# Seven products for the second matrix multiply of a gated feed-forward layer, in fifteen of its forty-eight blocks

## The chip, the core and the metric

The kernel runs on one core of one Trainium2 chip. The metric is the device time of one execution, in microseconds. Times that are compared are medians over several executions; a profile is of one execution.

## What is computed

A frequency filter along the sequence, then a normalisation by row and a gated feed-forward layer. The inputs are 8 sequences of 3008 rows of 256 numbers.

```python
X = np.fft.rfft(x, axis=1)
Y = X * (filt_r + 1j * filt_i)[None, :, :]
y = np.fft.irfft(Y, n=x.shape[1], axis=1)        # (8, 3008, 256)

x = y.reshape(24064, 256)
xn = x / np.sqrt(np.mean(x * x, axis=-1, keepdims=True) + 1e-06) * rms_g
g = xn @ w_gate                                  # 256 -> 1536
val = xn @ w_val                                 # 256 -> 1536
out = (g * (1 / (1 + np.exp(-g))) * val) @ w_out # 1536 -> 256
```

## The kernel before

**The feed-forward layer sets the beat.** A sequence b has six blocks m of up to four groups of 128 rows. A block has 12 slots, one for each piece jt of 128 of the 1536 hidden columns, so there are 8 x 6 x 12 = 576 slots in the list `items`. In a slot, `gv` (L533) makes gate and value of one hidden piece for all four row groups: two accumulating matmuls of 512 columns into pg, two into pv (L546), then SiLU on ScalarE (pg to sg, L550) and the product pv x sg on VectorE (hh, L551). pg and pv have two PSUM buffers each, hh has four buffers in turn. `down` (L554) then multiplies hh by w_out: for each of the four row groups one matmul of 256 columns with a 128 x 128 piece of hh as the weights (L563), accumulated over the 12 slots of the block in the two banks po0 and po1. At the block's end ScalarE and VectorE copy one bank each into o3 (L568, L569), and `o_store` sends it out from SP's queue.

**The filter is three stages of matmuls, spread over those slots.** For each sequence `a_unit` (12 units: matmul psa, copy to t1) is the first transform, and goes through DRAM (`z_store`, `t2_load`). The middle stage has 16 units: `b_unit` (four matmuls psb, then `s_part` on VectorE twice, the multiplication by the filter, L231 and L234), `add_unit` (GpSimd, the sum of the two parts, L268), `yt_load` (a transposing DMA on SP, one for two units) and `bi_unit` (four matmuls psi, ScalarE's copy to uu). `t4_load` transposes uu by DMA. The third stage goes by block: `n_unit` (matmul psn, ScalarE's copy to y), `sq_unit` (row sums of squares on ScalarE, L322), `stat_unit` (the factor rho, on GpSimd), `xt_unit` (GpSimd multiplies y's rows by rho, L340) and `tr_unit` (a transposing DMA on SP, which gives the block's xn).

**The order is written out by hand.** Every engine runs its instructions in the order in which the code issues them. The main loop issues for slot i: `gv` of slot i, then what the planner put into this slot, then `down` of slot i-2. The first `down` of a block is put off by one slot, and comes with the second, so that the banks can be emptied. The planner (`fit`, `norm_plan`, `a_plan`, `b_plan`) counts for each slot what it has put on ScalarE ("A"), VectorE ("V") and the two spare PSUM banks ("M", "B"), and moves a unit to a later slot until it fits. `b_at` gives the wished slots of the 16 middle units of sequence b, with t = 72 (b-1) the first slot of sequence b-1's blocks; `lags` say how much later `bi_unit` comes. The filter of sequence b thus runs in the slots of sequence b-1.

Staging buffers of 8 KB a partition (pool stg, four of them) hold filter and weights at the start, and later y, of which only half the buffer is used.

Of the kernel before, what the change touches and what calls it, by code (L numbers as in the profile page):

```python
# [10 lines left out]
FP32 = mybir.dt.float32  # L11
FP16 = mybir.dt.float16
AXT = mybir.ActivationFunctionType
ALU = mybir.AluOpType
# [6 lines left out]
P = 128  # L21
D = 256
B = 8
DFF = 1536
# [9 lines left out]
XC = 6  # L34
NXC = H // XC
KC = 8


def _make_tables():
# [62 lines left out]
def kernel(  # L102
# [21 lines left out]
    stg = ctx.enter_context(tc.tile_pool(name="stg", bufs=4))  # L124
# [27 lines left out]
    wg = glob.tile([P, 2, DFF], FP16)  # L152
    wv = glob.tile([P, 2, DFF], FP16)
    wo = glob.tile([P, JT, D], FP16)
    gsb = glob.tile([P, 2], FP32)
    hhs = [glob.tile([P, 512], FP16, name="hh%d" % i) for i in range(4)]
    ss3 = [glob.tile([P, 4, 2, P], FP16, name="ss%d" % i) for i in range(3)]
# [4 lines left out]
    seen = glob.tile([P, 4], FP16)  # L162

    st = {b: {"x": {}, "t1": {}, "t2": {}, "s": {}, "yt": {}, "t4": {}, "y": {}, "sq": {},
              "u": {}, "xn": {}} for b in range(B)}

    def raw(src, row, ap):
        return bass.AP(tensor=src.tensor, offset=src.offset + row * D, ap=ap)

    def y_tile():  # L170
        t = stg.tile([P, 2, 4, 256], FP32, tag="stg", name="y")
        return t.rearrange("p a b c -> p (a b c)")[:, 0:1024].rearrange("p (a e) -> p a e", a=2)

    def x_load(b, c):
        t = xp.tile([P, XC, D], FP16, tag="xc", name="xc")
# [127 lines left out]
    def nq(b, m):  # L303
        return 3 if (m == 5 and b % 2 == 0) else 4
# [30 lines left out]
    def xt_unit(b, m):  # L335
# [6 lines left out]
                                in1=rho[:, 0:n].unsqueeze(2).to_broadcast([P, n, D]), op=ALU.mult)  # L342
        st[b]["u"][m] = xt

    def tr_unit(b, m):
# [28 lines left out]
    FR4 = 4  # L374

    def f_load(i, f):
        if i not in fst:
            fst[i] = stg.tile([P, 2, FR4, D], FP32, tag="stg", name="fs")
# [134 lines left out]
    def scale_apply(m, bk):  # L513
# [12 lines left out]
                                    in1=y[:, h, :].rearrange("p (q e t) -> p q e t", q=2, e=2), op=ALU.mult)  # L526
        st[0]["xn"][m] = xn

    SPLIT = ((0, 0, 0), (B - 1, 5, JT - 1))
    hh_of = {}  # L530
    po_of = {}

    def gv(b, m, jt):  # L533
        n = nq(b, m)
        xn = st[b]["xn"][m]
        parts = ((0, 2), (2, 4)) if (b, m, jt) in SPLIT else ((0, n),)
        sg = hp.tile([P, 512], FP16, tag="sg", name="sg")
        hh = hhs[(6 * JT * b + JT * m + jt) % 4]
        made = []
        for q0, q1 in parts:  # L540
            w = (q1 - q0) * P
            pg = psG.tile([P, 512], FP32, tag="pg", name="pg")
            pv = psV.tile([P, 512], FP32, tag="pv", name="pv")
            for ps, wt in ((pg, wg), (pv, wv)):
                for dt_ in range(2):
                    nc.tensor.matmul(ps[:, 0:w], wt[:, dt_, ts(jt, P)], xn[:, q0:q1, dt_, :],  # L546
                                     start=(dt_ == 0), stop=(dt_ == 1))
            made.append((pg, pv, w, slice(q0 * P, q1 * P)))
        for pg, pv, w, c in made:
            nc.scalar.activation(out=sg[:, c], in_=pg[:, 0:w], func=AXT.Silu)  # L550
            nc.vector.tensor_tensor(out=hh[:, c], in0=pv[:, 0:w], in1=sg[:, c], op=ALU.mult)  # L551
        hh_of[(b, m, jt)] = hh
# [36 lines left out]

    def w_load(q):  # L590
        cols = ts(q, DFF // 3)
        t = stg.tile([P, 2, 2, DFF // 3], FP32, tag="stg", name="ws")
# [17 lines left out]
    with tc.manual_schedule():  # L610
# [142 lines left out]
        def norm_plan(b, m, slots, r):  # L753
            for i in range(2):
                s = fit(slots[i], ("M", 0, 1), ("A", 0, 0.6), ("A", 1, 0.82))
                at(s, n_unit, b, m, i)
                at(s + 1, sq_unit, b, m, i)
            for d, fn in zip(r, (stat_unit, xt_unit, tr_unit)):
                at(s + d, fn, b, m)
# [50 lines left out]
        for b in range(1, B):  # L810
            t = (b - 1) * 72
            if b == 1:
                z = a_plan(b, [i for i in range(12)])
                b_at, lags = [z + 7 + 7 * i // 5 for i in range(16)], (9, 9)
                soft = range(2, 16, 4)
            elif b == 2:
                z = a_plan(b, [28 + 3 * i for i in range(12)])
                b_at, lags, soft = [z + 13 + 7 * i // 3 for i in range(16)], (8, 9), ()
            else:
                at_ = [72 + 3 * i if b == 3 else t - 87 + 4 * i for i in range(12)]  # L820
                z = a_plan(b, [s - (s % JT == 1) for s in at_])
                b_at, lags, soft = [t - (25 if b == 3 else 26) + 4 * i for i in range(16)], (8, 12), ()
            assert z + 3 <= b_at[0] - 4
            end = b_plan(b, b_at, lags, soft)
            for c in range(4):
                at(end + 1 + (3 * c if b < 3 else c), t4_load, b, c)
            n_at = end + (4, 6, 8)[b] if b < 3 else t + (53 if b == 3 else 51)
            assert n_at >= end + 4
            for m in range(6):
                norm_plan(b, m, (n_at + 8 * m, n_at + 8 * m + (4 if b > 1 else 2)), (2, 3, 7) if b > 1 else (2, 3, 6))  # L830

        for i, now in plan.items():
            if any(fn == a_unit and a[3] == 0 for fn, a in plan.get(i + 1, ())) and bi_unit in [fn for fn, _ in now]:
                now.sort(key=lambda u: u[0] == sq_unit)

        stores = {}
        for i in range(len(items) + 4):
            if i < len(items):
                gv(*items[i])
            for fn, a in plan.pop(i, ()):  # L840
                fn(*a)
            if 2 <= i < len(items) + 2:
                b, m, jt = items[i - 2]
                if jt == 1 and i > JT:
                    down(b, m, 0)
                if jt or i < JT:
                    down(b, m, jt)
                if items[i - 2][2] == JT - 1:
                    stores[i + 1] = items[i - 2][:2]
# [35 lines left out]
```

## Time and profile before

| | |
|---|---|
| time, median of 3 runs (lowest, highest) | 863.48 us (862.96, 863.52) |
| span of the profiled execution, first to last instruction | 861.4 us |
| granted TensorE clock | 0.999 |
| instructions | 17024 |
| matmuls on TensorE | 6142 |
| data moved by DMA | 107.98 MB, 125 GB/s |
| ScalarE SiLU, L550, 128x512 | 595 ns each |
| VectorE product hh, L551, 128x512 | 691 ns each |
| VectorE filter products, L231 and L234, 128x384 | 547 and 546 ns each |
| GpSimd row scale, L340, 128x1024 | 1893 ns each |
| GpSimd sum of parts, L268, 128x384 | 911 ns each |

How to read it: engines are PE (TensorE's matmuls), PEld (its weight loads, which overlap the matmuls), DVE (VectorE), ACT (ScalarE), POOL (GpSimd) and SP (which only issues DMAs). A group's row has the line, the engine, the operation, what it writes and reads by the program's names, the shapes and the number of instructions; after the first bar the busy time in us and the mean length of one in ns; after the second the idle time of the engine just before them, and what ended it. A row in the order of time has start and length in us; where several instructions are merged, the length goes from the first one's start to the last one's end. A matmul's length includes the way through the array, so that one starts before the last has ended.

### The profile page before, as it was taken

To read this page: it belongs to the slowest core of one execution; us is meant where nothing else is said; L and a number is where in the kernel's file an instruction comes from. 1 tells how busy PE (TensorE), PEld (TensorE's weight loads), DVE (VectorE), ACT (ScalarE), POOL (GpSimd) and SP (SyncE) were. 2 spreads that over 40 slices of the span, in tenths; PEclk is the share of its full clock that TensorE was granted. 3 is DMA by queue.
4 is the path that set the end of the run, shared out by engine and by line. 5 is a ranking of instruction groups with operands and counts; after the bars stand their busy time and mean duration, and the time that the engine had idled before them with its cause. 6 is when DMAs were issued, how large, how long until landed. Compare 5 with 4: busy or idle time off the path is not lost.

```text
span 861.4 us, 17024 instructions
## 1 busy us (share of the span) xinstructions
PE 852.4 (99%) x6142; PEld 532.2 (62%) x6142; DVE 557.2 (65%) x926; ACT 612.4 (71%) x1339; POOL 297.8 (35%) x346
## 2 busy tenths in 40 slices
PE   8999999999999999999999999999999999999997
PEld 6755666566666666666666666666666666665664
DVE  5857655776666666666666676767666665555554
ACT  4986777787588756887577856888567765777443
POOL 5725742453144322534034430444123430132000
PEclk9999999999999999999999999999999999999999
DMA  9995778765975476656755548433564331521101
GB/s 283 270 204 124 150 164 168 139 130 121 197 137 129 121 150 111 151 107 147 139 127 113 132 98 180 108 87 101 131 127 93 97 70 42 124 54 49 62 25 50
DMA packets 198237, 107.98 MB, mean 125 GB/s; under 512 B 158566, under 2 KB 182520, under 8 KB 198152
## 3 DMA queue, kind: packets, MB, share of 16 engines
q1 hardware_dynamic: 189464, 85.52, 44.1%
q0 software_dynamic: 8544, 21.24, 12.7%
q8 instruction: 48, 0.79, 0.4%
q14 instruction: 37, 0.30, 0.1%
q10 hardware_dynamic: 144, 0.13, 0.0%
HBM read 45.78 MB, written 35.65 MB: 95 GB/s over the span
## 4 chain that ended last, share of the span: by engine, by line
PE 96%; DMA 1%; ACT 1%; DVE 1%; issue 0%; POOL 0%; POOLq 0%
PE po L563 28%; PE pg L546 28%; PE pv L546 28%; PE psb L241 3%; PE psi L285 3%; PE psn L314 2%; PE psa L206 2%; DMA fs<-in_filt_i_dram 1%; PE psy L418 1%; PE psf L389 1%; PE pst L367 0%; ACT sg L550 0%; POOL xc L186 0%; DVE s L231 0%; DVE hh L551 0%
## 5 line engine op out<-in xcount | busy, mean ns | idle before, releaser
L551 DVE TENSOR_TENSOR hh<-pv,sg 128x512 f16<-128x512 f32 (+2 forms) x578 | 391.5, 678 | 286.4 <-ACT sg L550 221.9
L550 ACT ACTIVATE sg<-pg 128x512 f16<-128x512 f32 (+2 forms) x578 | 337.4, 584 | 217.6 <-PE pg L546 213.4
L546 PE MATMUL pg<-xn,wg 128*128 128x512 f16 (+2 forms) x1156 | 338.1, 374 | 0.1
L546 PE MATMUL pv<-xn,wv 128*128 128x512 f16 (+2 forms) x1156 | 338.1, 374 | 0.0
L563 PE MATMUL po<-wo,hh 128*128 128x256 f16 x2256 | 332.7, 273 | 0.0
L563 PEld LDWEIGHTS <-hh 128*128 128x128 f16 x2256 | 213.4, 98 | 105.5 <-issue 0.6
L268 POOL TENSOR_TENSOR ss<-s,s 128x384 f16<-128x384 f16 x112 | 101.9, 911 | 273.2 <-DVE s L234 245.2
L546 PEld LDWEIGHTS <-wv 128*128 128x128 f16 x1156 | 112.9, 98 | 130.7
L546 PEld LDWEIGHTS <-wg 128*128 128x128 f16 x1156 | 111.4, 98 | 17.0 <-issue 0.3
L340 POOL TENSOR_TENSOR xt<-y,rho 128x1024 f16<-128x1024 f32 (+1 forms) x46 | 85.4, 1856 | 2.8
L322 ACT ACTIVATE junk<-y 128x256 f16<-128x256 f32 x180 | 74.3, 413 | 2.8
L231 DVE TENSOR_TENSOR s<-psb,ff 128x384 f16<-128x384 f32 x124 | 67.6, 547 | 0.7 <-ACT ff L195 0.6
L234 DVE TENSOR_TENSOR s<-psb,ff 128x384 f16<-128x384 f32 x124 | 67.6, 546 | 0.0
L195 ACT ACTIVATE uu<-psi 128x384 f16<-128x384 f32 (+1 forms) x127 | 61.6, 486 | 1.5 <-DMA out_dram<-o 0.5
L195 ACT ACTIVATE y<-psn 128x512 f32<-128x512 f32 (+1 forms) x95 | 55.7, 588 | 4.2
L285 PEld LDWEIGHTS <-yt 96*128 96x128 f16 x512 | 35.4, 97 | 26.7 <-issue 1.0
L332 POOL TENSOR_TENSOR rho<-u,mhalf 128x4 f32<-128x4 f32 (+1 forms) x46 | 46.5, 1010 | 3.8
L330 POOL TENSOR_SCALAR u<-ss 128x4 f32<-128x4 f32 (+1 forms) x46 | 8.9, 193 | 104.8 <-ACT junk L322 103.8
L195 ACT ACTIVATE t<-psa 128x512 f16<-128x512 f32 x70 | 41.4, 594 | 3.1 <-PE psa L206 1.7
L285 PE MATMUL psi<-wi,yt 96*128 96x96 f16 x512 | 42.9, 205 | 0.1
L241 PE MATMUL psb<-wb,t 96*128 96x96 f16 x480 | 40.1, 206 | 0.3 <-DVE s L234 0.2
L241 PEld LDWEIGHTS <-t 96*128 96x128 f16 x480 | 28.7, 97 | 12.8 <-DVE s L234 3.3
(101 smaller groups left out, 366.2 us busy)
## 6 DMA issues: line engine op xcount, KB each, us to landing
out_dram<-o SPq DMA_DIRECT2D x40, 512.0 KB, 3.6
xc<-in_x_dram POOLq DMA_DIRECT2D x31, 384.0 KB, 5.6
z_tmp<-t SPq DMA_DIRECT2D x28, 384.0 KB, 2.7
t<-z_tmp SPq DMA_DIRECT2D x28, 384.0 KB, 6.0
out_dram<-o SPq DMA_DIRECT2D x7, 384.0 KB, 2.7
fs<-in_filt_i_dram POOLq DMA_DIRECT2D x3, 512.0 KB, 10.8
fs<-in_filt_r_dram POOLq DMA_DIRECT2D x3, 512.0 KB, 11.2
ws<-in_moe_w_gate_dram POOLq DMA_DIRECT2D x3, 512.0 KB, 9.8
```

Source lines behind the costliest of these rows:

```text
L195: nc.scalar.activation(out=out, in_=in_, func=AXT.Copy, **({} if scale is None else {"scale": scale}))
L231: eng.tensor_tensor(out=o, in0=ps, in1=f1, op=ALU.mult)
L234: eng.tensor_tensor(out=o, in0=ps[:, :, ::-1, :], in1=f2, op=ALU.mult)
L241: nc.tensor.matmul(ps[:, ts(k, KR)], st[b]["t2"][kk // KC][:, kk % KC, ds(dh * P, P)], wb[0:KR, kk, :], start=True, stop=True)
L268: nc.gpsimd.tensor_tensor(out=ss3[g % 3][:, :, dh, 0:KR], in0=s[0], in1=s[1], op=ALU.add)
L285: nc.tensor.matmul(ps[:, k, :], yt[0:KR, k, dh, :], wi[0:KR, 4 * g + k, :], start=True, stop=True)
L322: nc.scalar.activation(out=junk, in_=y[:, i, ts(u, D)], func=AXT.Square, accum_out=ss[:, 2 * i + u:2 * i + u + 1])
L340: nc.gpsimd.tensor_tensor(out=xt[:, 0:n, :], in0=y.rearrange("p a (u d) -> p (a u) d", u=2)[:, 0:n, :], in1=rho[:, 0:n].unsqueeze(2).to_br ...
L546: nc.tensor.matmul(ps[:, 0:w], wt[:, dt_, ts(jt, P)], xn[:, q0:q1, dt_, :], start=(dt_ == 0), stop=(dt_ == 1))
L550: nc.scalar.activation(out=sg[:, c], in_=pg[:, 0:w], func=AXT.Silu)
L551: nc.vector.tensor_tensor(out=hh[:, c], in0=pv[:, 0:w], in1=sg[:, c], op=ALU.mult)
L563: nc.tensor.matmul(po[s4 // 2][:, s4 % 2, :], hh[:, ts(s4, P)], wo[:, jt, :], start=(jt == 0 and s4 % 2 == 0), stop=(jt == JT - 1 and (s4 ...
```

## The change

Fifteen blocks get another way through the second multiply: blocks 3 and 4 of the sequences 2 to 6, and blocks 0 to 4 of the last. With the row groups in two halves, `gv_seven` makes two hidden pieces for two row groups in a slot (eight matmuls of 256 columns, with twice the weight loads), SiLU and product as before. hh then holds a 2 x 2 matrix of 128 x 128 tiles, two row groups by two hidden pieces, and w_out's part a 2 x 2 matrix too. Strassen's method (seven products of sums of tiles in place of eight) needs sums of tiles of hh, which `sums` makes on VectorE, sums of tiles of w_out, which `w_seven` makes once on GpSimd, and sums of the products. `down_seven` has seven matmuls of 128 columns in a slot where `down` has four of 256. A half of the block is six slots; at its end results are put together on ScalarE, VectorE and GpSimd. The main loop issues `sums` of slot i-1 at the end of slot i, behind `down` of i-2.

```diff
+    big = [glob.tile([P, 2 * FR4 * D], FP32, name="big%d" % i) for i in range(4)]
+    spare = [t[:, FR4 * D:] for t in big]
+    half = [t.bitcast(FP16) for t in spare]
...
+    def xt_act(b, m, q):
+        rho = st[b]["u"][m]
+        y = st[b]["y"][m].rearrange("p a (u d) -> p (a u) d", u=2)
...
+        nc.scalar.activation(out=st[b]["xt"][m][:, q, :], in_=y[:, q, :], func=AXT.Copy, scale=rho[:, q:q + 1])
...
+    SEVEN = {(b, m) for b in range(2, B - 1) for m in (3, 4)} | {(B - 1, m) for m in range(5)}
+
+    def w_seven(n):
+        v = wo.rearrange("p (i j) (e d) -> p i j e d", j=2, e=2)
+        f, a, b = ((ALU.add, (0, 0), (1, 1)), (ALU.subtract, (0, 1), (1, 1)), (ALU.subtract, (1, 0), (0, 0)),
+                   (ALU.add, (0, 0), (0, 1)), (ALU.add, (1, 0), (1, 1)))[n]
+        nc.gpsimd.tensor_tensor(out=ws7[n], in0=v[:, :, a[0], a[1], :], in1=v[:, :, b[0], b[1], :], op=f)
+
+    def gv_seven(b, m, jt):
+        half, jp = divmod(jt, JP)
...
+        for ps, wt in ((pg, wg), (pv, wv)):
+            for j in range(2):
+                for dt_ in range(2):
+                    nc.tensor.matmul(ps[:, ts(j, 2 * P)], wt[:, dt_, ts(2 * jp + j, P)],
+                                     xn[:, 2 * half:2 * half + 2, dt_, :], start=(dt_ == 0), stop=(dt_ == 1))
+        nc.scalar.activation(out=sg, in_=pg, func=AXT.Silu)
+        nc.vector.tensor_tensor(out=hh, in0=pv, in1=sg, op=ALU.mult)
+
+    def sums(b, m, jt):
+        a = hh_of[(b, m, jt)].rearrange("p (s t) -> p s t", s=4)
...
+        nc.vector.tensor_tensor(out=hs[:, 0:2], in0=a[:, 0:2], in1=a[:, 3:4].to_broadcast([P, 2, P]), op=ALU.add)
+        nc.vector.tensor_tensor(out=hs[:, 2:4], in0=a[:, 1:3], in1=a[:, 0:4:3], op=ALU.subtract)
+        nc.vector.tensor_tensor(out=h5, in0=a[:, 0], in1=a[:, 2], op=ALU.add)
+
+    def down_seven(b, m, jt):
...
+        mm(pb[:, 0], a[:, 0], ws7[1][:, jp], **first)
+        mm(pb[:, 1], a[:, 3], ws7[2][:, jp], **mid)
+        mm(pa[:, 0], hs[:, 0], ws7[0][:, jp], **first)
+        mm(pb[:, 3], hs[:, 1], w[:, 0, 0], **mid)
+        mm(pa[:, 2], hs[:, 2], ws7[3][:, jp], **mid)
+        mm(pa[:, 1], hs[:, 3], ws7[4][:, jp], **last)
+        mm(pb[:, 2], h5, w[:, 1, 1], **last)
+        if jp == JP - 1:
+            o = o3_of[(b, m)][:, 2 * half:2 * half + 2, :].rearrange("p q (e d) -> p (q e) d", e=2)
+            t = osum
+            nc.scalar.activation(out=t[:, 4], in_=pa[:, 0], func=AXT.Copy)
+            nc.scalar.activation(out=t[:, 0:4], in_=pb, func=AXT.Copy)
+            nc.vector.tensor_tensor(out=o[:, 0:4:3], in0=pa[:, 1:3], in1=t[:, 4:5].to_broadcast([P, 2, P]), op=ALU.add)
+            nc.gpsimd.tensor_tensor(out=o[:, 1:3], in0=t[:, 0:2], in1=t[:, 2:4], op=ALU.add)
+            nc.gpsimd.tensor_tensor(out=t[:, 2:4], in0=t[:, 1::-1], in1=t[:, 2:4], op=ALU.subtract)
+            nc.gpsimd.tensor_tensor(out=o[:, 0:4:3], in0=o[:, 0:4:3], in1=t[:, 2:4], op=ALU.add)
...
         w_load(0)
-        w_load(1)
...
+        w_load(1)
         f_neg(4, 4, (0,))
...
+        for b, m in SEVEN:
+            for jt in range(JT):
+                load["V"][6 * JT * b + JT * m + jt] += 0.56
+            load["A"][6 * JT * b + JT * m + JP + 1] += 0.7
...
+            if fast:
+                for q in range(nq(b, m)):
+                    at(s + r[1] + 1 + q, xt_act, b, m, q)
+                    load["A"][s + r[1] + 1 + q] += 0.4
+                r = (0, 0, r[1] + 5)
+            else:
+                at(s + r[1], xt_unit, b, m)
...
-                b_at, lags, soft = [t - (25 if b == 3 else 26) + 4 * i for i in range(16)], (8, 12), ()
+                b_at, lags, soft = [t - 13 + 3 * i for i in range(16)], (8, 11), ()
...
+        for n in range(5):
+            at(96 + 10 * n, w_seven, n)
...
-                gv(*items[i])
+                (gv_seven if items[i][:2] in SEVEN else gv)(*items[i])
...
+                seven = (b, m) in SEVEN
+                fn, n = (down_seven, JP) if seven else (down, JT)
+                if jt % n == 1 and i > JT:
+                    fn(b, m, jt - 1)
+                if jt % n or i < JT:
+                    fn(b, m, jt)
+                if i - 1 < len(items) and items[i - 1][:2] in SEVEN:
+                    sums(*items[i - 1])
+                if jt == JT - 1:
+                    stores[i + (3 if seven else 1)] = (b, m)
```

So the middle stage of the sequences 3 to 7 has a unit every three slots (before, every four), from 13 slots ahead of t (before, 25 or 26), which puts nearly all of it ahead of the blocks 3 and 4. Where a block's row scale would fall into one of the fifteen blocks, `xt_act` does it on ScalarE in four multiplies, one a slot, and the transpose of the block's xn comes later by as much: this is so for 8 blocks. The staging pool becomes four plain buffers used in turn, and their upper halves, which y leaves free, hold the sums of tiles.

More of the change, by code (lines that the diff above doesn't have):

```diff
@@ L36 @@
 KC = 8
+FR4 = 4
 def _make_tables():
@@ L154 @@
     wo = glob.tile([P, JT, D], FP16)
+    big = [glob.tile([P, 2 * FR4 * D], FP32, name="big%d" % i) for i in range(4)]
+    spare = [t[:, FR4 * D:] for t in big]
+    half = [t.bitcast(FP16) for t in spare]
+    ws7 = [half[n // 2][:, ts(n % 2, JT // 2 * P)].rearrange("p (i d) -> p i d", d=P) for n in range(5)]
+    hs4 = [(half[0][:, 1536:], half[1][:, 1536:], half[3][:, 0:512], half[3][:, 512:1024])[i]
+           .rearrange("p (s t) -> p s t", s=4) for i in range(4)]
+    hs1 = [half[3][:, 1024 + i * P:1024 + (i + 1) * P] for i in range(4)]
+    osum = spare[2][:, 384:1024].rearrange("p (s t) -> p s t", s=5)
     gsb = glob.tile([P, 2], FP32)
@@ L164, with big_tile @@
     st = {b: {"x": {}, "t1": {}, "t2": {}, "s": {}, "yt": {}, "t4": {}, "y": {}, "sq": {},
-              "u": {}, "xn": {}} for b in range(B)}
+              "u": {}, "xn": {}, "xt": {}} for b in range(B)}
     def raw(src, row, ap):
         return bass.AP(tensor=src.tensor, offset=src.offset + row * D, ap=ap)
+    turn = [0]
+    def big_tile():
+        turn[0] += 1
+        return big[(turn[0] - 1) % 4]
     def y_tile():
-        t = stg.tile([P, 2, 4, 256], FP32, tag="stg", name="y")
-        return t.rearrange("p a b c -> p (a b c)")[:, 0:1024].rearrange("p (a e) -> p a e", a=2)
+        return big_tile()[:, 0:FR4 * D].rearrange("p (a e) -> p a e", a=2)
     def x_load(b, c):
@@ L343, in xt_unit @@
         st[b]["u"][m] = xt
+    def xt_act(b, m, q):
+        rho = st[b]["u"][m]
+        y = st[b]["y"][m].rearrange("p a (u d) -> p (a u) d", u=2)
+        if q == 0:
+            st[b]["xt"][m] = xtp.tile([P, 4, D], FP16, tag="xt", name="xt")
+        nc.scalar.activation(out=st[b]["xt"][m][:, q, :], in_=y[:, q, :], func=AXT.Copy, scale=rho[:, q:q + 1])
+        if q == nq(b, m) - 1:
+            st[b]["y"].pop(m)
+            st[b]["u"][m] = st[b]["xt"].pop(m)
     def tr_unit(b, m):
@@ new lines, in gv_seven @@
+    def gv_seven(b, m, jt):
+        half, jp = divmod(jt, JP)
+        xn = st[b]["xn"][m]
+        sg = hp.tile([P, 512], FP16, tag="sg", name="sg")
+        hh = hhs[(6 * JT * b + JT * m + jt) % 4]
+        pg = psG.tile([P, 512], FP32, tag="pg", name="pg")
+        pv = psV.tile([P, 512], FP32, tag="pv", name="pv")
+        for ps, wt in ((pg, wg), (pv, wv)):
[5 more added lines that the diff above has]
+        nc.vector.tensor_tensor(out=hh, in0=pv, in1=sg, op=ALU.mult)
+        hh_of[(b, m, jt)] = hh
@@ new lines, in sums @@
+    def sums(b, m, jt):
+        a = hh_of[(b, m, jt)].rearrange("p (s t) -> p s t", s=4)
+        n = (6 * JT * b + JT * m + jt) % 4
+        hs, h5 = hs4[n], hs1[n]
+        nc.vector.tensor_tensor(out=hs[:, 0:2], in0=a[:, 0:2], in1=a[:, 3:4].to_broadcast([P, 2, P]), op=ALU.add)
+        nc.vector.tensor_tensor(out=hs[:, 2:4], in0=a[:, 1:3], in1=a[:, 0:4:3], op=ALU.subtract)
+        nc.vector.tensor_tensor(out=h5, in0=a[:, 0], in1=a[:, 2], op=ALU.add)
+        hh_of[(b, m, jt)] = (a, hs, h5)
@@ new lines, in down_seven @@
+    def down_seven(b, m, jt):
+        a, hs, h5 = hh_of.pop((b, m, jt))
+        half, jp = divmod(jt, JP)
+        if jt == 0:
+            o3_of[(b, m)] = op.tile([P, 4, D], FP32, tag="o3", name="o3")
+        if jp == 0:
+            po_of[(b, m)] = [psO.tile([P, 2, D], FP32, tag="po%d" % i, name="po%d" % i)
+                             .rearrange("p a (e d) -> p (a e) d", e=2) for i in range(2)]
+        pa, pb = po_of[(b, m)]
+        first, mid, last = dict(start=(jp == 0), stop=False), dict(start=False, stop=False), \
+            dict(start=False, stop=(jp == JP - 1))
+        w = wo[:, 2 * jp:2 * jp + 2, :].rearrange("p j (e d) -> p j e d", e=2)
+        mm = nc.tensor.matmul
+        mm(pb[:, 0], a[:, 0], ws7[1][:, jp], **first)
[14 more added lines that the diff above has]
+            nc.gpsimd.tensor_tensor(out=o[:, 0:4:3], in0=o[:, 0:4:3], in1=t[:, 2:4], op=ALU.add)
+            po_of[(b, m)] = o3_of[(b, m)]
@@ L529 @@
     SPLIT = ((0, 0, 0), (B - 1, 5, JT - 1))
+    o3_of = {}
     hh_of = {}
@@ L591, in w_load @@
         cols = ts(q, DFF // 3)
-        t = stg.tile([P, 2, 2, DFF // 3], FP32, tag="stg", name="ws")
+        t = big_tile().rearrange("p (k e j) -> p k e j", k=2, e=2)
         for src, k in ((moe_w_gate, 0), (moe_w_val, 1)):
@@ L757, in norm_plan @@
                 at(s + 1, sq_unit, b, m, i)
-            for d, fn in zip(r, (stat_unit, xt_unit, tr_unit)):
-                at(s + d, fn, b, m)
+            fast = items[s + r[1]][:2] in SEVEN
+            at(s + r[0], stat_unit, b, m)
+            if fast:
[5 more added lines that the diff above has]
+                at(s + r[1], xt_unit, b, m)
+            at(s + r[2], tr_unit, b, m)
             assert s + r[-1] + 1 < 72 * b + 12 * m
@@ L843 @@
                 b, m, jt = items[i - 2]
[L844 to L849, printed above, removed]
+                seven = (b, m) in SEVEN
[8 more added lines that the diff above has]
+                    stores[i + (3 if seven else 1)] = (b, m)
             for fn, a in late.pop(i, ()):
```

5 lines of the change are left out of this document (2 added, 3 removed).

## The prediction

> **What bounds the kernel now.** I read the page's busy shares and its chain first.
>
> ```profile
> PE 852.4 (99%) x6142; PEld 532.2 (62%) x6142; DVE 557.2 (65%) x926; ACT 612.4 (71%) x1339; POOL 297.8 (35%) x346
> ...
> PE 96%; DMA 1%; ACT 1%; DVE 1%; issue 0%; POOL 0%; POOLq 0%
> ```
>
> TensorE is busy and is the chain; other engines matter only where one makes it wait. Next, one slot in the order of time (start, length):
>
> ```profile
> 609.97 0.69 DVE L551 TENSOR_TENSOR hh<-pv,sg 128x512 f16<-128x512 f32 x1
> 610.01 0.59 PE L546 MATMUL pg<-xn,wg 128*128 128x512 f16 x2
> 610.44 0.60 PE L546 MATMUL pv<-xn,wv 128*128 128x512 f16 x2
> 610.64 0.60 ACT L550 ACTIVATE sg<-pg 128x512 f16<-128x512 f32 x1 [0.70 <-PE pg L546]
> 610.87 0.60 PE L563 MATMUL po<-wo,hh 128*128 128x256 f16 x4
> 611.27 0.69 DVE L551 TENSOR_TENSOR hh<-pv,sg 128x512 f16<-128x512 f32 x1 [0.61 <-ACT sg L550]
> ```
>
> The next pg starts at 611.31, so a slot is 1.30 us. A 512-column matmul takes 0.216 (610.01 to 610.44 is two), a 256-column one 0.109 ((0.60 - 0.273)/3): 4 x 0.216 + 4 x 0.109 = 1.30. From pg's start to SiLU is 0.63, from SiLU to hh another 0.63. `down` uses an hh two slots old, so these latencies cost nothing now. Then, what the new instructions can be priced by, from the groups by shape:
>
> ```profile
> L551 DVE TENSOR_TENSOR hh<-pv,sg 128x512 f16<-128x512 f32 x526 | 363.3, 691 | 265.9 <-ACT sg L550 207.3 <-PE psn L314 28.9 <-PE psa L206 13.4
> ...
> L551 DVE TENSOR_TENSOR hh<-pv,sg 128x256 f16<-128x256 f32 x4 | 1.6, 422 | 1.0 <-ACT sg L550 0.8 <-PE pg L546 0.2
> ...
> L197 DVE COPY t4f<-pst 128x512 f16<-128x512 f16 x1 | 0.4, 425 | 0.5 <-PE pst L434 0.5
> ...
> L510 DVE TENSOR_TENSOR hl<-rho,hl 128x4 f16<-128x4 f32 x1 | 0.2, 163 | 0.0
> ```
>
> VectorE takes 1.05 ns an element from fp32 ((691 - 422)/256) over about 0.158 fixed, but 0.52 from fp16 ((425 - 158)/512). An operation that waits for nothing starts before the last has ended:
>
> ```profile
> 500.77 0.69 DVE L551 TENSOR_TENSOR hh<-pv,sg 128x512 f16<-128x512 f32 x1
> 501.38 0.55 DVE L231 TENSOR_TENSOR s<-psb,ff 128x384 f16<-128x384 f32 x1
> ```
>
> 0.61 from start to start, 0.08 less than the length. And the two places that show 128-column matmuls with a weight load each, and a load that waits for VectorE:
>
> ```profile
> 47.59 0.65 PEld L483 LDWEIGHTS <-t 128*128 128x128 f16 x8
> 47.80 0.61 PE L483 MATMUL psn<-tab,t 128*128 128x128 f16 x8
> ```
>
> ```profile
> 23.31 1.02 DVE L231 TENSOR_TENSOR s<-psb,ff 128x384 f16<-128x384 f32 x2 [0.64 <-ACT ff L195]
> ...
> 23.92 0.17 PEld L418 LDWEIGHTS <-s 128*96 128x96 f16 x2 [1.03 <-DVE s L231]
> 23.92 0.26 PE L418 MATMUL psy<-tab,s 128*96 128x128 f16 x1 [0.79 <-DVE s L231]
> ```
>
> Eight take 0.61, the last 0.219 of it: (0.61 - 0.219)/7 = 0.056 each. The first multiply ends at 23.31 + 0.55 = 23.86, the load starts 0.05 later, and its matmul lasts 0.26 where others last 0.22: 0.09 from VectorE's end to useful work.
>
> **The change, part by part.** The sum is made against the profiled execution, 861.4 us; the median of the runs, 863.5, lies 2.1 above it, which I add at the end.
>
> *TensorE's columns.* In a seven-product slot gate and value are 8 matmuls of 256 columns, 0.872, and seven products of 128 are 7 x 0.056 = 0.392: 1.264 in place of 1.300. Fifteen blocks are 180 slots: 180 x 0.036 = -6.5 us, the most there is to gain.
> [...]
>
> *Operand sums.* VectorE gets two additions of 256 fp16 elements and one of 128 per slot, SBUF to SBUF. No row shows that form. At fp16's 0.52 they last 0.158 + 0.134 = 0.292 and 0.225; at fp32's 1.05, 0.427 and 0.292. I take the fp16 end: the nearest row with fp16 in and out is L197's. Less 0.083 of overlap they take 0.209 + 0.209 + 0.142 = 0.56; with hh's 0.61 VectorE has 1.17 of 1.264, so it fits as a sum. In time it doesn't. The code issues hh of slot i ahead of the sums of i-1, and `down_seven(i-1)` comes one slot later, behind that slot's gate and value. From the start of slot i: gate's fourth matmul ends 3 x 0.109 + 0.272 = 0.60; SiLU starts at 0.64, hh at 1.27 (+0.63), the sums at 1.88 (+0.61); the last ends 0.418 + 0.225 later, 2.52, and its matmul can run at 2.61. TensorE gets to that matmul at 1.264 + 0.872 + 6 x 0.056 = 2.47. So it waits 0.14; that lengthens the slot, so the next sum is in time: 0.14 every second slot.
>
> *Half blocks.* Results now leave PSUM every 6 slots, not 12. The postponed pair of `down`s gives TensorE two slots' gates in a row, and VectorE has no such gap: counted from the slot with the half's last product, hh issues 1.27 to 1.88; the new addition out of PSUM (256 elements, 0.422 - 0.083 = 0.34) waits for ScalarE's first copy, to 2.25; sums to 2.81. ScalarE's copies (128 and 512 elements: 0.28 and 0.595, overlapping by 0.1) start at 1.60, when the last product lands, so SiLU starts at 2.28 and hh at 2.90; the sums end at 4.15, usable at 4.24. TensorE wants them at 1.40 + 2 x 0.872 + 0.392 + 0.336 = 3.87: 0.37 late. With the waits in the other slots (the fourth and the sixth of the half) a half loses 0.37 + 2 x 0.14 = 0.64 and gains 6 x 0.036 = 0.22: +0.42, by 30 halves **+12.6 us**.
>
> *Costed at nothing.* ScalarE's row scale: 8 blocks, 32 multiplies of 256 (0.41 each by L322) in place of 8 GpSimd ones of 1.89; between two SiLUs ScalarE has 0.7 idle (the slot above). Uncovered: 32 x 0.41 = 13 us. Other planned work in these slots (15 groups of psi at 0.17, 16 of psn at 0.22) gives VectorE time while its copies take some of ScalarE's: -3 to +3, taken as 0. The middle stage at three slots a unit, with its transposes and loads on SP in the same order: the planner put batch 2's at 7/3 slots before, and there TensorE hardly waited:
>
> ```profile
> 150.00:205.00 55.00, 54.89 (x404) 33.05 (x403) 39.49 (x68) 42.85 (x97) 27.61 (x29) 1.00 0.63 128
> ```
>
> 0.11 idle in 55 bounds five batches (36 slots each, 234 us) to +0.5; uncovered, each of 80 units could hold TensorE for one s multiply, 0.46: 37 us. Five weight sums on GpSimd (768 elements; L340 takes 1466 ns for as many), ten slots apart, sit in its idle 65%; late, they would hold an add, the yt transpose behind it on SP and psi, 8 us in all. The store on SP now waits three slots for GpSimd, and t4 and yt loads queue behind it; psi has five slots, 6.5 us, against yt's 3.2 to land. The second weight load keeps its place in GpSimd's queue.
>
> Sum: 861.4 + 12.6 = 874.0, + 2.1 = **876 us**. Its own range is 867 to 885: 0.05 us a slot either way over 180 slots.
>
> **Rivals.**
> 1. *The sums wait behind GpSimd.* After each half GpSimd makes three dependent additions of 256 fp32 elements; L340's 1893 ns for 1024 and 1466 for 768 give 1.67 an element, 0.61 each. If an addition keeps VectorE's two-input SBUF operations waiting, one met in the two groups of sums there holds everything behind it: 30 x 0.61 = 18, so **894**. For it: the adds fall on those sums. Against it: nothing shown; VectorE has no such two-input pair at work beside GpSimd before.
> [...]
> 2. *A rate binds.* Sums at 1.05 an element take 0.90, VectorE 1.51 + 0.34/6 = 1.56 a slot: 180 x 0.26 = +47, **911**. Seven loads of 0.098 uncovered (0.69 for 0.39) come to the same. Against: L197's fp16 copy; L483's 56 ns.
> 3. *The sums are ready in time* (faster). Place: the last sum of each slot, 0.14 late in a chain of 2.6, and the 0.37 at the half. If the chain to it is shorter by these, by a smaller fixed part (a 4-element memset takes 62 ns) and a SiLU not held by the copies, only the columns count: 861.4 - 6.5 + 2.1 = **857**. It decides from waits under 0.22 a half.
> 4. *It cancels*: the fixed part alone shrinks to 62. The steady wait goes, the half's falls to about 0.25: 30 x (0.25 - 0.22) = +1, **864**.
>
> **Chances.** Forecast 0.46, port 0.20, rate 0.06, in time 0.20, cancels 0.08. A measurement of this kernel can tell 0.2%, 1.7 us: faster 0.20, same 0.08, slower 0.72. The range 857 to 897 takes in 3 and 4 and most of 1, and leaves out 2 and 1's upper part.
>
> **What would show it.** Seven matmuls of 128 columns in 0.39 us when not held; sums of 0.29 and 0.22 us; idle TensorE ended by VectorE's sums, some 0.6 us a half, most behind the postponed pair; blocks without seven products unchanged. Sums far longer where GpSimd's additions run would show rival 1; sums of 0.43 rival 2; a TensorE without waits in those blocks makes the prediction wrong.

## The result, and the profile after

| | before | after |
|---|---|---|
| time, median of 4 runs | 863.45 us | 905.82 us (904.80 to 907.31) |
| ratio, 95% interval | | 1.0494 (1.0481 to 1.0507) |
| span of the profiled execution | 861.4 us | 904.1 us |
| granted TensorE clock, mean | 0.999 | 0.997 |

The changed kernel is slower by 42.4 us, above the predicted range of 857 to 897. Shares and chain of its page:

```profile
PE 868.2 (96%) x7402; PEld 603.9 (67%) x7402; DVE 679.0 (75%) x1477; ACT 632.8 (70%) x1420; POOL 361.6 (40%) x433
...
PE 76%; DVE 12%; ACT 5%; issue 4%; DMA 2%; SPq 1%; POOL 0%; ACTq 0%; DVEq 0%; POOLq 0%
```

VectorE holds 12% of the chain, where it had 1%. GpSimd is not in the chain at all, although, as will be seen, it causes most of the loss: it doesn't release TensorE, it lengthens what VectorE does. Who makes TensorE wait (total us, times, longest), from the view of waits:

```profile
PE po L600 <- DVE big L580: 11.2, 27, 0.5
PE po L602 <- DVE big L581: 8.1, 15, 1.6
PE po L604 <- DVE big L582: 5.5, 13, 0.6
```

L580 to L582 are the three operand sums; L598 to L604 are the seven products. The groups by shape:

```profile
L581 DVE TENSOR_TENSOR big<-hh 128x256 f16<-128x256 f16 x180 | 67.4, 374 | 0.0
L582 DVE TENSOR_TENSOR big<-hh 128x128 f16<-128x128 f16 x180 | 52.3, 290 | 0.0
L580 DVE TENSOR_TENSOR big<-hh 128x256 f16<-128x256 f16 x180 | 51.7, 287 | 0.0
...
L611 POOL TENSOR_TENSOR o<-big 128x256 f32<-128x256 f32 x30 | 24.0, 801 | 134.1 <-ACT big L609 134.1
L613 POOL TENSOR_TENSOR o<-o,big 128x256 f32<-128x256 f32 x30 | 23.0, 768 | 2.4
L612 POOL TENSOR_TENSOR big<-big 128x256 f32<-128x256 f32 x30 | 22.8, 760 | 2.4
```

L580 (an addition) and L581 (a subtraction) have the same shape and follow each other at once, yet one takes 287 ns on average and the other 374. The end of a half in the order of time shows why (the products' weight loads and some matmuls are left out):

```profile
803.25 0.43 DVE L610 TENSOR_TENSOR o<-po,big 128x256 f32<-128x256 f32 x1 [0.18 <-ACT big L608]
...
803.60 0.28 DVE L580 TENSOR_TENSOR big<-hh 128x256 f16<-128x256 f16 x1
803.73 0.75 POOL L611 TENSOR_TENSOR o<-big 128x256 f32<-128x256 f32 x1 [9.02 <-ACT big L609]
803.79 0.84 DVE L581 TENSOR_TENSOR big<-hh 128x256 f16<-128x256 f16 x1
...
804.56 0.79 POOL L612 TENSOR_TENSOR big<-big 128x256 f32<-128x256 f32 x1
...
804.69 0.68 DVE L573 TENSOR_TENSOR hh<-pv,sg 128x512 f16<-128x512 f32 x1
...
805.29 0.28 DVE L580 TENSOR_TENSOR big<-hh 128x256 f16<-128x256 f16 x1
805.43 0.72 POOL L613 TENSOR_TENSOR o<-o,big 128x256 f32<-128x256 f32 x1
805.49 0.81 DVE L581 TENSOR_TENSOR big<-hh 128x256 f16<-128x256 f16 x1
805.62 0.23 PE L600 MATMUL po<-big,big 128*128 128x128 f16 x1 [0.46 <-DVE big L580]
...
806.36 0.23 PE L602 MATMUL po<-big,big 128*128 128x128 f16 x1 [0.45 <-DVE big L581]
```

L581 begins 0.06 us after GpSimd's first addition, and lasts 0.84 in place of 0.28, to 0.15 after the addition's end. The same happens with the third addition. The second runs beside hh (L573), which reads PSUM and one SBUF operand, and hh keeps its 0.68. TensorE, which has two slots' products in a row here, waits for L580 and then for L581.

**An account of the 42.7 us of span.** I add up, over all pairs of successive matmuls, what lies from start to start beyond 0.216, 0.109 and 0.056 us for 512, 256 and 128 columns (0.163 for 384). Before, these waits are some 3 us after the start-up; after, they are 37.5 in the fifteen blocks and 14.8 in the others. 37.5 + 11.8 more, less 6.3 of saved columns, is 43.0. A block counts here from its first gate matmul to that of the next block, so the products of its last two slots fall into the block behind it: of the 14.8 us, 8.0 are still waits of seven-product matmuls, which wait 45.5 us in all.

Most of the loss stands in one place. The two slots of a block that hold the postponed pair are 2.57 and 3.03 us long on average, and 1.73 and 1.72 without the sums (experiment 3). The products of these slots wait 31.5 us in all. In the six halves that follow no additions, because a normal block stands in front, it is 0.33 to 0.35 us each; in the other 24 halves it is 0.82 to 1.36.

### The profile page after: what moved, and what is told of

Same layout as the page of the kernel before. It is cut to its first block, busy times and chain, and to the rows that moved or that the text cites. A ratio compares the mean times of both kernels' runs of the same rounds, so it can differ in the third digit from the quotient of the medians.

```text
span 904.1 us, 20300 instructions
## 1 busy us (share of the span) xinstructions
PE 868.2 (96%) x7402; PEld 603.9 (67%) x7402; DVE 679.0 (75%) x1477; ACT 632.8 (70%) x1420; POOL 361.6 (40%) x433
## 4 chain that ended last, share of the span: by engine, by line
PE 76%; DVE 12%; ACT 5%; issue 4%; DMA 2%; SPq 1%; POOL 0%; ACTq 0%; DVEq 0%; POOLq 0%
PE po L651 17%; PE pg L634 17%; PE pv L634 17%; PE pg L570 5%; PE pv L570 4%; PE psb L254 2%; ACT sg L572 2%; DVE hh L573 2%; DVE big L582 2%; DVE big L581 2%; PE psi L298 2%; PE psa L219 2%; PE psn L327 2%; DVE big L580 1%; PE po L602 1%
## 5 line engine op out<-in xcount | busy, mean ns | idle before, releaser
L639 DVE TENSOR_TENSOR hh<-pv,sg 128x512 f16<-128x512 f32 (+2 forms) x398 | 267.2, 672 | 181.7 <-ACT sg L638 140.0
L638 ACT ACTIVATE sg<-pg 128x512 f16<-128x512 f32 (+2 forms) x398 | 230.4, 580 | 128.0 <-PE pg L634 124.5
L634 PE MATMUL pg<-xn,wg 128*128 128x512 f16 (+2 forms) x796 | 231.5, 372 | 0.1
L634 PE MATMUL pv<-xn,wv 128*128 128x512 f16 (+2 forms) x796 | 231.5, 372 | 0.0
L651 PE MATMUL po<-wo,hh 128*128 128x256 f16 x1536 | 227.3, 272 | 0.0
L281 POOL TENSOR_TENSOR ss<-s,s 128x384 f16<-128x384 f16 x112 | 102.6, 917 | 206.0 <-DVE s L247 189.5
L572 ACT ACTIVATE sg<-pg 128x512 f16<-128x512 f32 x180 | 107.5, 597 | 105.7 <-PE pg L570 94.4
L573 DVE TENSOR_TENSOR hh<-pv,sg 128x512 f16<-128x512 f32 x180 | 123.7, 687 | 24.2 <-ACT sg L572 20.0
L570 PE MATMUL pg<-xn,wg 128*128 128x256 f16 x720 | 108.0, 273 | 0.0
L570 PE MATMUL pv<-xn,wv 128*128 128x256 f16 x720 | 108.0, 273 | 0.0
L634 PEld LDWEIGHTS <-wg 128*128 128x128 f16 x796 | 76.3, 98 | 11.4 <-issue 0.3
L611 POOL TENSOR_TENSOR o<-big 128x256 f32<-128x256 f32 x30 | 24.0, 801 | 134.1 <-ACT big L609 134.1
L335 ACT ACTIVATE junk<-big 128x256 f16<-128x256 f32 x180 | 74.7, 415 | 2.8
L581 DVE TENSOR_TENSOR big<-hh 128x256 f16<-128x256 f16 x180 | 67.4, 374 | 0.0
```

Of the source, the lines that this page charges most:

```text
L281: nc.gpsimd.tensor_tensor(out=ss3[g % 3][:, :, dh, 0:KR], in0=s[0], in1=s[1], op=ALU.add)
L335: nc.scalar.activation(out=junk, in_=y[:, i, ts(u, D)], func=AXT.Square, accum_out=ss[:, 2 * i + u:2 * i + u + 1])
L570: nc.tensor.matmul(ps[:, ts(j, 2 * P)], wt[:, dt_, ts(2 * jp + j, P)], xn[:, 2 * half:2 * half + 2, dt_, :], start=(dt_ == 0), stop=(dt_ = ...
L572: nc.scalar.activation(out=sg, in_=pg, func=AXT.Silu)
L573: nc.vector.tensor_tensor(out=hh, in0=pv, in1=sg, op=ALU.mult)
L581: nc.vector.tensor_tensor(out=hs[:, 2:4], in0=a[:, 1:3], in1=a[:, 0:4:3], op=ALU.subtract)
```

## The experiments

In the order in which they were run; the waits are counted as above.

| kernel | time, us | ratio to before (95%) | waits in the fifteen blocks / others, us |
|---|---|---|---|
| the changed kernel | 905.8 | 1.0494 (1.0481, 1.0507) | 37.5 / 14.8 |
| GpSimd's adds left out | 880.9 | 1.0199 (1.0184, 1.0215) | 13.2 / 13.7 |
| memsets in their place | 881.1 | 1.0202 (1.0187, 1.0217) | 13.2 / 14.2 |
| no operand sums | 859.6 | 0.9954 (0.9939, 0.9969) | 0.1 / 5.8 |
| sums in their hh's slot | 883.1 | 1.0225 (1.0208, 1.0242) | 21.5 / 7.3 |
| middle stage where it was | 916.3 | 1.0614 (1.0596, 1.0632) | 50.4 / 12.6 |
| row scale all on GpSimd | 911.9 | 1.0562 (1.0546, 1.0578) | 47.0 / 11.3 |
| three slots behind | 881.8 | 1.0212 (1.0197, 1.0227) | 8.7 / 19.3 |
| the same, no adds | 871.0 | 1.0089 (1.0074, 1.0104) | 0.4 / 17.6 |
| three behind in the fifteen only | 876.5 | 1.0156 (1.0141, 1.0172) | 9.2 / 13.9 |
| the same, adds paced | 867.2 | 1.0049 (1.0036, 1.0061) | 1.4 / 12.3 |
| two behind, adds paced | 881.5 | 1.0210 (1.0196, 1.0224) | 16.8 / 11.4 |
| sums behind the drain | 878.7 | 1.0179 (1.0165, 1.0193) | 17.0 / 8.5 |
| three behind, paced, bank awaited | 864.5 | 1.0013 (1.0004, 1.0022) | 1.4 / 11.4 |

**1. GpSimd's three additions left out.**

```diff
-            nc.scalar.activation(out=t[:, 0:4], in_=pb, func=AXT.Copy)
-            nc.vector.tensor_tensor(out=o[:, 0:4:3], in0=pa[:, 1:3], ...)
-            nc.gpsimd.tensor_tensor(out=o[:, 1:3], ...)
-            nc.gpsimd.tensor_tensor(out=t[:, 2:4], ...)
-            nc.gpsimd.tensor_tensor(out=o[:, 0:4:3], ...)
+            nc.scalar.activation(out=o, in_=pb, func=AXT.Copy)
+            nc.vector.tensor_tensor(out=t[:, 0:2], in0=pa[:, 1:3], ...)
```

> Left out: GpSimd's three additions at the end of each half (ScalarE's second copy goes straight into the output buffer, VectorE's addition into the scratch), so all else runs as in the changed kernel. Theory A, exclusion: an operand sum, with two inputs in SBUF, and a GpSimd addition that reads SBUF can't run together. Then the second sum's mean falls from 374 ns to about 290, TensorE's wait behind the postponed pair from about 1.3 us to 0.4, and the time by 30 x 0.9 = 27 us to about 879. Theory B, order alone: the waits come from hh being issued ahead of the sums, GpSimd's work beside them is chance; then the time stays at 906, within 3 us.

880.9: the additions cost 24.9 us. The sums take 281, 310 and 218 ns, and the waits at the postponed pairs fall from 31.5 to 7.3 us, while the six halves without additions in front keep their 0.33 to 0.35. The seven products still wait 21.3 us in all. Of this 5.0 us stand at five products behind sums that other GpSimd work lengthens as before: one row scale, and four times L281, the sum of the two filter parts.

**2. Three memsets of 512 elements in place of the additions**, 0.52 us each, which only write.

```diff
+            for _ in range(3):
+                nc.gpsimd.memset(t[:, 0:4], 0.0)
```

> As the run without additions, but with three GpSimd memsets of 512 fp32 elements in their place: GpSimd is at work at the same moments, and only writes SBUF. Theory A, if the shared thing is a way to read: as without the additions, about 879, sums of 290 ns. If any GpSimd work beside them holds the sums: more than 890, with long second sums. Theory B: 906.

881.1, as without anything. The memsets lie on the same sums:

```profile
787.41 0.28 DVE L580 TENSOR_TENSOR big<-hh 128x256 f16<-128x256 f16 x1
787.55 0.53 POOL L612 MEMSET big<- 128x512 f32 x1 [9.03 <-DVE big L610]
787.61 0.28 DVE L581 TENSOR_TENSOR big<-hh 128x256 f16<-128x256 f16 x1
787.81 0.22 DVE L582 TENSOR_TENSOR big<-hh 128x128 f16<-128x128 f16 x1
```

So it isn't GpSimd's being busy that holds the sums (L581 takes 0.28 here, 0.84 beside an addition): what the memsets lack against the additions is the reading of SBUF.

**3. No operand sums**; the products take hh's own tiles.

```diff
-        nc.vector.tensor_tensor(out=hs[:, 0:2], ...)
-        nc.vector.tensor_tensor(out=hs[:, 2:4], ...)
-        nc.vector.tensor_tensor(out=h5, ...)
-        hh_of[(b, m, jt)] = (a, hs, h5)
+        hh_of[(b, m, jt)] = (a, a, a[:, 0])
```

> Left out: the operand sums; the seven products take hh's tiles themselves. Both theories: no wait is left in the fifteen blocks, and only the columns count: 180 x 0.036 = 6.5 us less than the kernel before, about 857 to 858. Above 861 would mean that the columns themselves cost more than the 0.056 and 0.109 us of the profile before.

859.6, with 0.1 us of waits in the fifteen blocks. This is what the columns alone are worth: 3.8 us, being 6.3 in the blocks less 2.6 of new waits elsewhere (with rounding). All the rest of the loss comes with the sums: 21.2 us without GpSimd's additions (880.9 - 859.6), 24.9 more with them.

**4. The sums in the slot of their own hh**, right behind it, not one slot later.

```diff
+                if items[i][:2] in SEVEN:
+                    sums(*items[i])
...
-                if i - 1 < len(items) and items[i - 1][:2] in SEVEN:
-                    sums(*items[i - 1])
```

> The sums directly behind the same slot's hh in VectorE's order, as they would stand without the change's 'one slot later'. Theory A: the half's end stays bad; in the other slots VectorE now waits for its own hh, 0.13 us a slot, while the sums come a slot earlier for TensorE: between 895 and 915. Theory B: the sums are ready a slot ahead of their matmuls, the waits vanish: below 875.

883.1, outside both numbers: 22.7 us gained though the additions remain and hold the sums still (means of 334, 308 and 273 ns). What TensorE waits for is something else now:

```profile
PE po L600 <- DVE o L610: 15.7, 24, 1.1
```

A sum that is ready a slot earlier can be held without harm, but L610, which empties bank po0, stands in VectorE's queue behind the held sums, and the next half's first product into that bank waits. So holding is a delay, and what it costs depends on the slack of whatever is queued behind it.

**5. The middle stage back in its old places.**

```diff
-                load["V"][6 * JT * b + JT * m + jt] += 0.56
+                load["V"][6 * JT * b + JT * m + jt] += 0.0
...
-                b_at, lags, soft = [t - 13 + 3 * i for i in range(16)], (8, 11), ()
+                b_at, lags, soft = [t - (25 if b == 3 else 26) + 4 * i for i in range(16)], (8, 12), ()
```

> The middle stage's instructions go back to the places they had before (its parts 4 slots apart, not 3, and spread into the fifteen blocks); all else as in the changed kernel. The move costs nothing, as I predicted: 900 to 912 us, within 6 us of 905.8, since the waits of the normal blocks in which the middle stage now lies are 0.01 to 0.02 us. If instead the closer spacing is part of the 42 us that are lost, the time falls below 895. If the move shelters the fifteen blocks from work that would hold VectorE and ScalarE there, the time rises above 912.

The first pair of lines takes the sums out of the planner's count for VectorE, so that the units aren't moved away from these places. 916.3: 10.5 us slower, above the window of no cost. L281 also reads two SBUF operands. With the stage back among the fifteen blocks 16 of its 112 instructions lie on a sum, and each makes that sum 0.99 to 1.02 us long; in the changed kernel it is 4. Placing the stage ahead of the blocks shelters the sums.

**6. The row scale on GpSimd everywhere** (`fast = False`).

> The row scale of the fifteen blocks goes back from ScalarE (2 x 0.50 us a tile) to GpSimd (one multiply of 128x1024, 2.05 us in block (2,5), next to which an operand sum took 1.98 us in place of 0.28). Theory A, that GpSimd's reads of SBUF hold the sums back: 16 more such multiplies, each holding one sum for some 1.7 us of which TensorE feels 1 to 1.7: +16 to +27 us, 922 to 933. Rival, that ScalarE's 501 ns halves make the SiLUs late: the time falls to 895 to 903.

911.9: 6.1 us slower, in neither window. The expectation counted 16 tiles; the multiply's rows show 46 in place of 38, eight. Nine sums lie beside such a multiply, where the changed kernel has one, and are held for 11.7 us in all; the waits in the fifteen blocks grow by 9.5 us, and those in the others fall by 3.5.

**7. Products three slots behind gate and value** (a fifth set of hh and sum tiles, and for its room three buffers of sg in place of four), additions as they are.

```diff
...
-            if 2 <= i < len(items) + 2:
-                b, m, jt = items[i - 2]
+            if 3 <= i < len(items) + 3:
+                b, m, jt = items[i - 3]
...
```

> The products run three slots behind the gate and value matmuls in place of two (a fifth set of hh and sum tiles), so each sum has one slot of 1.26 us more; GpSimd's adds stay. Latency theory (a sum held back by about 0.5 us costs only because the chain to the products has no slack): the waits mostly go, 864 to 872. Rate theory (the held sums take VectorE's time itself: 7.34 us a half plus 1.05 us of holding, from 31.5 us over 30 halves, against TensorE's 7.58): 0.81 us a half stays, 24 us above a kernel with no waits (about 860): 880 to 888. If the waits come from neither, 900 or more.

**8. The same without the additions.**

> Three slots behind as in the kernel before this one, and GpSimd's three adds left out (the output's combinations are not formed, so its values differ). The run without adds at two slots took 880.9 with waits of 13.2 us in the fifteen blocks. If those waits are the sums' lateness by order, as I predicted (0.14 every second slot, 0.37 at each half), the extra slot takes them all: 860 to 866. If VectorE's rate holds the blocks even without adds, 872 or more.

881.8 lies in the rate theory's window and 871.0 between the two, but the waits decide otherwise. In the fifteen blocks the latency theory holds: with one more slot the waits fall from 37.5 to 8.7 us, although the sums are held for 25 us still; without the additions they fall from 13.2 to 0.4. VectorE's rate is not the limit there. But the others' waits grow to 19.3 and 17.6, which put both times above what the theory gave; 4.6 us is one wait for a load from z_tmp that the later order delays, the rest is spread.

**9. Three slots behind in the fifteen blocks only**, two elsewhere.

> Three slots behind in the fifteen blocks alone, two elsewhere; GpSimd's adds as in the changed kernel. With three slots everywhere the time was 881.8, of which the fifteen blocks waited 8.7 us and the other blocks 19.3 (4.6 of it one wait for a load from z_tmp), against 5.8 in the kernel without sums (859.6). If those others come from the normal blocks' extra slot: 859.6 + 8.7 + 2 to 5 = 868 to 874. If they come from VectorE being behind after each of the fifteen blocks, they stay: 879 to 884.

876.5, between the two. The wait for z_tmp is down to about 1 us; 4.8 us stand now between a gate matmul and the first normal product behind a seven-product block.

**10. The same, and GpSimd's additions paced:** six of 128 columns, one a slot, each waiting for that slot's last sum, so that it lies beside hh. The tile of block (2,5) is scaled on ScalarE as well, and a block's output is stored three slots later.

```diff
...
+            if pend:
+                made = pend.pop(0)()
+                if 1 <= i <= len(items) and items[i - 1][:2] in SEVEN:
+                    tc.add_manual_dep(made.ins, last_sum[0].ins.name, ...)
...
```

> As the kernel before this one, and GpSimd's three adds of 256 columns a half become six of 128, one a slot, each waiting for that slot's last operand sum, so that it runs while VectorE makes hh out of PSUM; the row scale of a tile that falls in the slot after a block of the fifteen goes to ScalarE too. Theory A with the sums' slack (nothing but SBUF reads of GpSimd beside a sum is left of the loss): sums back at 281, 281 and 214 ns, waits in the fifteen blocks below 2 us, 859.6 + 0 to 4 = 859 to 864, by 0 to 0.5% faster than before. Rival, that the added waits and GpSimd's queue make the output stores or the other sums late, or that 128-column adds still reach into the next sum: 866 to 875.

867.2. The sums' means are short again, though nine of the 540 still lie on an addition and take up to 0.54 us:

```profile
L581 DVE TENSOR_TENSOR big<-hh 128x256 f16<-128x256 f16 x180 | 51.0, 283 | 0.0
L580 DVE TENSOR_TENSOR big<-hh 128x256 f16<-128x256 f16 x180 | 50.9, 283 | 0.0
```

and a slot looks like this, the addition under hh:

```profile
782.79 0.68 DVE L573 TENSOR_TENSOR hh<-pv,sg 128x512 f16<-128x512 f32 x1
783.01 0.45 POOL L611 TENSOR_TENSOR big<-big 128x128 f32<-128x128 f32 x1 [0.75 <-DVE h5x L582]
783.39 0.28 DVE L580 TENSOR_TENSOR big<-hh 128x256 f16<-128x256 f16 x1
```

Waits in the fifteen blocks are 1.4 us, as theory A expected; the time is in the rival's window, because of 12.3 us outside them, 6.0 of which stand at the first two products of a normal block behind a seven-product one.

**11. Paced additions alone**, two slots behind as in the changed kernel, with the output stored four slots later.

> The changed kernel with two slots as it is, and only GpSimd's adds paced under hh (six of 128 columns). If the loss that the adds cause is their overlap with the sums, and not their number or their traffic, the time is that of the run without adds: 878 to 884. If adds that don't overlap cost as much, 900 or more.

881.5, within 0.6 us of the time without additions (880.9): what the additions cost, they cost by lying on the sums.

**12. The sums in their own slot, behind L610.**

```diff
-                if i - 1 < len(items) and items[i - 1][:2] in SEVEN:
-                    sums(*items[i - 1])
...
+            if i < len(items) and items[i][:2] in SEVEN:
+                sums(*items[i])
             for fn, a in late.pop(i, ()):
```

> The operand sums in the slot of their own hh as in the run of 883.1, but behind that slot's products, so that VectorE's add out of PSUM (0.41 us) stands ahead of them. In that run 19.6 of its 21.5 us of waits were the second product of a half waiting for the bank that this add frees, the add being behind sums which GpSimd held back. Order theory: that wait goes, 862 to 868. Rate theory: VectorE needs 0.72+0.21+0.20+0.13 = 1.26 us a slot when a sum follows its own hh at once, and 0.41 + 0.7 a half besides, against TensorE's 7.58 a half: it stays short, 880 to 890.

878.7, in neither window. The wait for L610 is gone, and others stand in its place (4.7 us for L582, 2.3 for hh): by the view of waits VectorE is now late with the sums themselves and with hh. Why the total hardly falls was not taken apart further.

**13. As 10, with the first two products of the normal block behind a seven-product block one slot later**, so that their bank has been emptied.

```diff
-                if jt % n == 1 and i > JT:
-                    fn(b, m, jt - 1)
-                if jt % n or i < JT:
+                k = 2 if not seven and (b, m - 1) in SEVEN else 1
+                if jt % n == k and i > JT:
+                    for j in range(k):
+                        fn(b, m, jt - k + j)
+                if jt % n >= k or i < JT:
```

> As the kernel of 867.2 (paced adds, three slots behind in the fifteen blocks), with one thing moved: in the normal block behind a block of the fifteen the first two products wait one slot more and come as three together, so the bank they write has been emptied. Bank theory: the 867.2 holds 12.3 us of waits outside the fifteen blocks, of which 4.4 + 1.7 us stand between a gate matmul and the first two normal products behind a block of seven products; they go: 861 to 863, by 0 to 0.25% faster than before. Rival, that VectorE is simply behind at the end of each such block: the waits come back one slot later, 865 to 868.

864.5, between the two. The waits at that bank fall from 6.0 to 1.3 us, the time by 2.8; in the profiled execution single waits for loads (1.3 us for yt, 1.4 for z_tmp) stand in the filter's matmuls instead. At 1.0013 (1.0004 to 1.0022) it is not ahead of the kernel before. No kernel here that makes the sums is.

## Why the prediction was wrong

The failed step is the choice, under the rivals, to leave the exclusion between VectorE and GpSimd out of the sum ("Against it: nothing shown") and to give it 0.20. The forecast had this term at nothing. The runs show 24.9 us for the additions, most of the 29.8 us between the forecast of 876 and the 905.8 measured, and some 5 more for sums that other GpSimd work holds. The prediction's own steps against the runs, in the span's order:

| step | predicted | measured |
|---|---|---|
| columns | -6.5 us | -6.3 in the blocks |
| the sums' lateness by order (30 halves) | 30 x 0.64 = +19.2 | 30 x 0.42, the median half of run 1, = +12.6 |
| other waits of the seven products without the additions | 0 | +8.6, of which 5.0 behind sums held by a row scale and by L281 |
| exclusion by GpSimd's additions | 0 in the forecast, +18 in rival 1 | +24.9 |
| other blocks | 0 | +2.6 |

These sum to 42.4. The second and third rows are together the 21.2 us between runs 1 and 3; that this lies so near the predicted 19.2 is luck, since the order's part was a third smaller and the rest was not foreseen. Taken as the forecast, rival 1 would have given 894; the 11.8 us beyond it are 6.9 of its own price, 2.0 in the second and third rows, 2.6 in the other blocks and 0.2 of columns (with rounding).

- **Columns: right.** Seven products go out 0.056 us apart when not held; in the profile of after L600 to L603 start at 802.31, 802.37, 802.42 and 802.48.
- **Lengths of the sums: right.** 0.28, 0.28 and 0.216 where nothing holds them, against 0.292, 0.292 and 0.225; rival 2 (fp32's rate, 0.43) is excluded.
- **The half blocks: right in mechanism, too large in size, without GpSimd.** Behind the postponed pair 0.37 was predicted, and 0.22 to 0.35 measured in most halves without additions; in the other late slots it was 0.14, and 0.08 measured. In the changed kernel the pair's slot holds 0.82 to 1.36 us of waits wherever additions run in front of it: this is the term of the sum that the exclusion breaks.
- **Rival 1: right in kind and place, its price short by 7 us.** It took 0.61 an addition and one met a half, for 30 halves. On average an addition lasts 0.76 to 0.80, two of three meet a sum, and only 24 halves follow additions, each of which loses about 1.0 us: of the 31.1 us by which sums are lengthened in the profile of after, 13.1 lie beside L611, 12.2 beside L613, 1.2 beside L612. Pacing (11) and leaving out (1) take the same 24 to 25 us away, and writes alone (2) leave the time at 881.1 against 880.9. The same sum, with two inputs in SBUF, takes 0.84 us beside an addition that reads SBUF and 0.28 beside a memset that only writes it. Not every GpSimd instruction that reads SBUF held a sum: the power on 128x4 held none (last section).
- **Costed at nothing: the row scale on ScalarE** costs at most the 1.4 us that the fifteen blocks still wait in experiment 10, and moving it back costs 6.1. One tile that stayed on GpSimd, in the first slots of block (2,5), held a sum for 1.98 us and TensorE for 1.61:

```profile
347.12 2.05 POOL L353 TENSOR_TENSOR xt<-big,rho 128x1024 f16<-128x1024 f32 x1
...
347.33 1.98 DVE L581 TENSOR_TENSOR big<-hh 128x256 f16<-128x256 f16 x1
...
349.37 0.23 PE L602 MATMUL po<-big,big 128*128 128x128 f16 x1 [1.61 <-DVE big L581]
```

- **The middle stage: free where most of it lies now**, as predicted (by the count above some 0.02 us a slot in the normal blocks, the seven products that end there left out), but not neutral: it keeps L281 off the sums, worth 10.5 us (5).
- **Rivals 3 and 4:** the sums were not in time by themselves; with no sums at all the time is 859.6, near rival 3's 857, and with a third slot of distance and no additions the fifteen blocks get there (0.4 us of waits).

What stays open: why the blocks outside the fifteen keep some 6 us more waits in 10 and 13 than without sums. One bank was part of it in 10; what is left in 13 is spread over single waits, mostly of the filter's matmuls. The three buffers of sg and the later stores came with these kernels and were not tested by themselves. It is also open what the 3.6 us of the third row that no held sum explains are.

## What to carry to other kernels

Before giving work to an idle engine, ask what it shares: three additions a half on a GpSimd that was 35% busy cost 25 us where they read SBUF beside VectorE's additions from SBUF, and memsets in their place left the time at 881.1, against 880.9 without either; paced to lie beside an operation out of PSUM the additions came to 881.5. A delay of half a microsecond costs what the slack behind it doesn't absorb, so look at the queue behind the delayed instruction, and give a new link in a chain its own slot of distance. And where the code puts two operations side by side that no row shows side by side, their clash is not the unlikely case because nothing is shown of it.

## What the runs showed of the hardware

- A sum held by GpSimd ends 0.08 to 0.15 us after GpSimd's instruction: it lasts 0.84 beside an addition (0.75), 1.02 beside L281 (0.91), 1.98 beside the row scale (2.05). A GpSimd power of 128x4 that takes 1.08 us held none of the sums beside it (780.13 in experiment 10; they took 0.28).
- In the changed kernel TensorE's granted clock fell to half for 3.4 us, behind a stretch of 4 us in which TensorE was busy for 2.05. The table by stretches of the profile of after (TensorE's busy time stands third, its clock third from the end):

```profile
347.00:351.00 4.00, 2.05 (x17) 1.04 (x15) 4.00 (x8) 1.54 (x4) 2.63 (x3) 1.00 0.34 32
351.50:354.00 2.50, 2.42 (x13) 1.42 (x14) 1.66 (x6) 2.02 (x7) 1.13 (x2) 0.53 0.26 54
```

  Two matmuls of 384 columns take 0.84 us there, and 0.49 at 349.57. Block (2,5) waits 4.8 us in all, 1.6 of it for the sum beside the row scale, 0.7 for one beside L281, and 1.6 at the half clock. Such waiting did not always go with a lower clock: without the additions (run 1, mean clock 0.999) TensorE is busy for 2.00 of the 4 us from 344.2 to 348.2, with waits for the same two sums, and the clock is 1.00 there and behind. What decides it is not shown.
